# Attention with routed experts on one core: ScalarE copies 114 of 288 score half units out of PSUM

## The chip, the cores and the metric

One Trainium2 chip, one of its cores. The metric is the device time of one execution in microseconds (us). The kernel is one launch.

## The reference, cut to what matters

```python
# q, k, v: (8, 8, 576, 64) = batch, heads, tokens, head size
q_rot, k_rot = rotate(q), rotate(k)                 # rotary position
scores = 1/sqrt(64) * q_rot @ k_rot^T
attn = exp(scores - max(scores)) / (sum + 1e-9)
x = (attn @ v), heads joined                         # (8, 576, 512)
# per batch:
s = x @ w_gate                                       # one gate score a token
top = the 128 tokens with the highest s
y = relu(x[top] @ w1) @ w2                           # 512 -> 1024 -> 512
out = x;  out[top] = x[top] + sigmoid(s[top]) * y
```

## The kernel before

Work is cut into 16 **groups**: a batch and four of its eight heads. A group has 18 **half units**: `c` is one of two head pairs, `u` one of nine blocks of 64 queries. The two heads of a pair lie on the upper and lower 64 partitions, so a half unit's scores are 128 partitions x 576 keys. They fill two PSUM banks (a "wide"), 288 columns in each. There are eight banks, so at most four half units' scores stand in PSUM at a time.

For each half unit TensorE makes the scores (`units`, 16 matmuls for two half units). In `softmax` VectorE reads them out of PSUM, multiplies by -1/8, writes the negated scores to the `prob` tile in SBUF and keeps the minimum of each row in `nm`: one instruction. ScalarE then applies the exponential in place in `prob`, with the minimum as bias, and sums the rows. VectorE transposes `prob` in blocks of 32 x 32, mostly two half units at once. When all 18 half units of a group are transposed, TensorE makes the **value products** (`value`, three parts of 96 matmuls), which need four banks. Their output goes to `ot`, is transposed on TensorE, scaled by the row sums into `x`, and stored. The `prob` tile has two copies, so a group's scores can be made while the previous group's are in use.

After every second group the batch is routed: gate products on GpSimd, totals on VectorE or ScalarE, ranks of the tokens (`route`), a gather of 128 rows by indirect DMA, two expert layers on TensorE (`products`, 8 parts a batch), and an indirect DMA back. GpSimd also rotates `q_in` and `k_in`.

**Order.** Nothing is scheduled on the chip: each engine runs its instructions in a fixed order. Every operation has a number, and `LINES` holds, for each of the five queues, the numbers in order, two characters each. `Order.run` walks these five lists with its own costs to fix the order of issue and which banks each operation gets; `issue` emits the instructions with their semaphores. A bank is given to a next user when the last reader of the old one has ended. TensorE's operations have a mode (`mode` 0, 1, 2: tile shapes of 128 x 128, 32 x 64, 64 x 64); neighbours of different mode cost a change.

Line numbers in the profile are those of the helper that records every call (L236), so groups are told apart by tile names: `prob<-banks` is the read-out with the minimum, `prob<-prob,nm` the exponential, `prob<-prob` the transposition, `banks<-k_in,q_in` the scores, `banks<-prob,vt` the value products.

Of the kernel before, what the change touches and what calls it, by code (L numbers as in the profile page):

```python
# [27 lines left out]

LINES = {
    "PE": """  # L30
010P0H0X1b131j1r1x1D0T171n0-1f0L2B2R2J2F2V2x2-2N1J351K3b1L3h3n5d4L1Q4R1U1S575j4X515p5v3t3u3v6n6h6t3E3A6F3C6R6z6L6X715B4a
5C5D4h5I5K8h8n8t4k5M778z788F798R8L7i4n7e7g8X919P4r4s9V9-4u7Ia54vahab97an98at99azbP9e7Pb-bV4xc54y9i9g4z7Scb4AaFchaGcnaHct
czaOaMdl7VaQdxdr7Z7+dDcFdJcGdPcHdVflcMcOcQbe80d-81e5fr83bl84fx85bofD86fPfJebfVecf-edg5gTembrekeigZh3gbh9gchfgdhrhlgigkgm
bvhxbwiTiZbyeMbzhDj3eTbBj9bCeWjfbDjlbEhJjrhKjxhLjDkpeZhQhUhSkNkHkBkvjJkTjKkZjLl3mpjQf1jSjUf2l9mviif4mBf5mNmHf7ipf8mTf9is
famZlfn3lgn9lhnXlmivlolqnfo1ngo7nhojodnolQnqnmizopiAoviCpXiDoBlXiFq1iGoHl+iHq7iIqdoNqjoOqpoPqvqBoWoUoYm1qHrlm5rrm6rDrxpm
m8rJm9rPrVqNr-qOs5qPptmbqUqWmcqYpwsbscsdmdsisksmpzmepDsxpGpEsEpJsHpHpKpLsKpMsOsPsRsUsSsVsWsX""",
    "ACT": """
02030R0J0Z1d151l1t1v1B1F1z0V19111p1H1h0N2D2L1O2T2H2X2Z2z312P3339373f3d1M1N3j3l3p3r1R3y1V1T4N594T5h5f5n5l4P4-4Z5t1+5r4V5b
5z55535x203w3x5G226p6r6j3B6l3F6J3D6x6V6H3K6T6N3M6Z6v3O6-6P756D6B735E5F5J8r8x7c8p4p8l8j8v8B8D8H8J5U7b7a4o5W8V8N8P8T8Z957o
8-9T934t7q7s9ca39X9R4wa1a79Zafarapajada99b9aavax9faBaDc3al9jc7aKc1bXbZbR9qcfbT7Xcdc9cjclcpcraJaIcxaPcD7WdpcvdBcBdzdn7-dv  # L40
cKdtdHdFdNaYdLdTdRcJcIdXa+cPdZcRfpcW82e3fncYe1e9fte7egfvfBfzbtfHc+fFfTfLfNfRfZfXg3g1eeefg9g7enbselg-gXggh1gVh7h5hdhbeuew
hhhjgfgehvhthphnglhBgsiVgui-j1bAiXhHhzhFj7jdjbe-j5jjhOjpjhjnjvjtjBjzhNhMjHjFe+hTktkLkJkDkRkPkrkzkFkxkVjOk-l1jNjMkXl7i0l5
jTmtf3mzmxlbldmrj+f6mDmFmRk0lkmJmLmVmPn1m-ixmXn5n7nbndljlinkiwnZn-lwlAo3o5o9obnjninpofoholnniBonoxotozorp-iEpZnwoDoFoLoJ
nyoSqbqfm3q5q9qhq3qlqnqtqroRoQqzqxoXm2qDqFp2rpp4rnqLrvm7rzqJqSrtrFrLmarNrHrZrBrXrRs1s3s9rTs7qQqRqZqVr2sgpBser4pApFpIsMsT""",
    "DVE": """
0r0s0v0w0t0u0z0x0A0y0C0Q0I0Y0S1c140+1k160K1m1e1s1u1y1A1w1E1G180U1o101g1C0M0W1I1a1q2C0O2S1i2K2G2Y2W122y322U2O302M2E2+3836
2Q2A342I3e3c3a3g3k3i3q3o1P5e5g4O3s4M4U4S3m585a3z5k5m4Y4+54525s5q5o5w5y5i5u505c4W4Q566q6o6k6i6w6s6u6G6I5A6m6S6U6A6C6O6M6+
6Y74725H6W496K4e6y4d4c4g706Q4f6E4i765L8k8i8o8q8w5N8u4l7d8s5S8m8C8A8y8G8I8E4q8K8U8S8O7j8M7f7h8+8Y948Q9Q9S9290969Y9Wa07Ha2
8W7M7Na8a67L7O7Kaiak9+aeaca4aq9dao9UasagauawaaaCaAbQbS7Qc0bYbWaEc2c8c6ay9ham9occceb+7T4Bc4bUckcgci9scacocqcmcsaLcwcucCaN
cAdoaR7YdmdAcydudydsaWcEdCdGdEdqdIdMdKdwdSdQdOdUcLdWdYfobdfmcNbibhd+e0e2bjbkbge8fsfue4e6bmfqeafyehfwbpfAfGfE87fSbufMfKfQ  # L50
fIfCfWfYfUf+g2g0fOg4g8g6gUgWgaejg+h0esh4h6h2hahcgYh8hghihehkeLhuhsghhogjhmgnhwhqhyhAbxiWj0iUi+eSeQeReOePgwhEhGj6j4eUj2iY
jahCjcjgeXjihIjojebFjmf0j8jkjujsjqjAjyhPjwjCjGjEkskqjIhVhRkQkOkKkIkEkCkykwkMh+kSkWkUkGjPkuk+l0kAl2l6l4mskYjRjVi2mqihl8lc
lamymwikimiliniomCmEmumQmAmIlemKiqirmMmOmUmWk2itllfbm+mSn0mGn4n6mYn2nanciyn8nenYlnlrn+lpo2o4lyo0o8lPoaocomokognloelSlWnr
lUlTlVoioso6owoyoqoop+pYoAoCoEoulYq0q4oGoKoIl-q2oMq8qaiJqeqgnAqcqmqkq6qiqsqqoTqoquqyqwqEqCoZoVqAqIqKroqGrmrsrup6rqplrGrE
rArypspppoprrMrKpqqMrSrQrYrIrWm4rwr+s0s2rOs8qTrCs6s4purUsaqXpxshsfsjsnr6soslspsqsssrswpCmfszsDsAsCsBsFsGsIsLpNsQsNsY""",
    "POOL": """
0B0F0D0E0G2p2v2q2t2w2u2r2s4D4E4J4F4G4H4K4I6f696g1Z6a6b6d1-6c6e218b898a8c3J8d3L3N8f8e9H8g4b9L4j5R9M9N4m5T9O9I5V9J9K7n7p7r
7JbHbNbJbLbIbKbMbO7Rddde9n9pdjdh9rdi7UdfdgdkaVfjfk4CfdfeaXfffhfifgaZcVbfcXcZbnbqgNgOgLgPgRgSgQgM88eretiRiPeviLiQiNiOiMiS
greNgtgveVknkoeYkhkjkiklkmkkbGmhhZmnmimjmkmomlmmh-i1ijjZj-k1nRnVnSiunPnTnUnQnWfcpRlvlxlzpSpTpUpVlRpPpQpWnvlZnxnzm0rjrdrk
rfiKrhrergrip1p3p5pnpvr1r3pyr5symgsJpOsZ""",  # L60
    "SP": """
04060508070a090c0b0n0m0k0e0j2i0h0q0p0g2f0o0d3-2g0l232c2k26282a25240f29413X0i2j2d272b422n403V3Q3W3Y3S003P2m2l2o3R3T3U5+43
5-5X5Y5Z2h631X3Z6144483+601W62461Y453I7t7u477x3H7y7A64657w7z66685O7v3G672e7B7D7C5P7E5Q7l7k9u9A9y9z9v9t9w9C9x7F7m7G9E9D9G
9Bb0b3a-9Fb6b1b4b2b59kb7ba9l9mbbb9bcb8d2d6d5d0c-d7d1d3aUaTd4dcaSeFdad8cTcSeGezdbeAexeDd9cUeEeCeyeBeHeKeIgDgCgBgEeJgyeqgz
gxepgAgKgIgHiceogGgJgFi7iai9i4gqi5i6i3i8goieibiggpk4k3kak5k9k6kbifidhWk7k8kclKlJjXhYlDlBkflHlIlEkglCkehXkdlFjWlGlOlNnFnD
nElLlMnInCnHnBnGjYnJltpfnLntpgnKlunOnMlspepdnNpap8p7p9pbpcp0phpinso-r7pjpknur8rar9rcrbr0o+stq-q+susv""",
}


# [951 lines left out]
```

## Time and profile before

| | us |
|---|---|
| time, median of 3 runs | 520.5 (520.34 to 521.34) |
| the profiled execution's own time | 521.84 |
| its span (first to last instruction) | 520.1 |
| TensorE busy | 486.8 (94%) |
| VectorE busy | 453.1 (87%) |
| ScalarE busy | 327.1 (63%) |
| GpSimd busy | 340.3 (65%) |

PE is TensorE's matmuls, PEld its weight loads, DVE is VectorE, ACT ScalarE, POOL GpSimd, SP the engine that issues most DMAs. The end of a matmul is modelled, so a busy PE is not PE at its peak. The duration of an instruction holds its latency: the next one on the same engine can begin before it ends, so what one costs is read from start to start.

### The profile page before, as it was taken

The page shows a single profiled execution, that of the slowest core. Times are in us where ns is not written, and L with a number is a line of the kernel's source. Part 1 is how long each engine was busy: PE and PEld are TensorE (multiplying, and loading weights), DVE is VectorE, ACT ScalarE, POOL GpSimd, SP SyncE. Part 2 cuts the span into 40 slices and gives each one's busy share as a digit, 9 for nine tenths or more (in the row PEclk, how much of TensorE's full clock was granted, in tenths as well). Part 3 has the DMA queues.
Part 4 walks back from the last instruction along what each step waited for, and adds up shares of the span by engine and source line. Part 5 has one row for each costly group of instructions (what it writes and reads, how often), then busy time and mean ns, then how long its engine had stood idle before and what let it go on. Part 6 is the DMA issues. An engine that isn't in the chain of part 4 may idle for free. (4 is left out here: it accounts for less than half of the span.)

```text
span 520.1 us, 18964 instructions
## 1 busy us (share of the span) xinstructions
PE 486.8 (94%) x7988; PEld 300.1 (58%) x7988; DVE 453.1 (87%) x988; ACT 327.1 (63%) x965; POOL 340.3 (65%) x268
## 2 busy tenths in 40 slices
PE   8779897899999999999899998999999999999995
PEld 7336354455665456655557454574657556666873
DVE  7999999998998999999989989999959989992710
ACT  0666898847847768685686657775657668764000
POOL 3989299698495889658687597727778397014110
PEclk9999999899999999999999999999999999999999
DMA  8884567367545465254452547246464243121310
GB/s 293 273 249 139 176 208 232 105 186 219 162 134 150 128 177 192 84 171 140 159 167 80 182 133 226 74 119 191 149 203 120 69 149 114 52 64 49 107 41 20
DMA packets 47381, 76.52 MB, mean 147 GB/s; under 512 B 4928, under 2 KB 28224, under 8 KB 47296
## 3 DMA queue, kind: packets, MB, share of 16 engines
q1 hardware_dynamic: 45472, 70.54, 44.2%
q0 software_dynamic: 1280, 4.20, 2.3%
q8 instruction: 62, 1.02, 0.9%
q10 hardware_dynamic: 544, 0.59, 0.4%
q14 instruction: 23, 0.19, 0.2%
HBM read 63.77 MB, written 11.53 MB: 145 GB/s over the span
## 5 line engine op out<-in xcount | busy, mean ns | idle before, releaser
L236 ACT ACTIVATE prob<-prob,nm 128x576 f32<-128x576 f32 x288 | 221.1, 772 | 115.1 <-DVE prob L236 114.8
L236 DVE TENSOR_SCALAR_CACHE_REDUCE prob<-banks 128x576 f32<-128x576 f32 x288 | 204.3, 745 | 16.1 <-PE banks L236 14.1
L236 PE MATMUL banks<-k_in,q_in 64*64 64x288 f32 x2304 | 181.9, 417 | 22.5 <-DVE prob L236 8.9
L236 DVE STREAM_TRANSPOSE prob<-prob 128x1152 f32<-128x1152 f32 (+1 forms) x153 | 193.7, 1287 | 5.7 <-ACT prob L236 5.6
L236 PE MATMUL banks<-prob,vt 32*64 32x288 f32 x4608 | 150.9, 405 | 2.4 <-ACT prob L236 0.9
L236 PEld LDWEIGHTS banks<-k_in,q_in 64*64 64x64 f32 x2304 | 81.8, 133 | 109.4 <-DVE prob L236 28.7
L236 PEld LDWEIGHTS banks<-prob,vt 32*64 32x64 f32 x4608 | 98.9, 132 | 51.5 <-issue 12.6
L236 POOL TENSOR_TENSOR k_in<-k_in,tabk 128x1152 f32<-128x1152 f32 (+1 forms) x31 | 80.9, 2613 | 17.7 <-DMA k_in<-k_dram 15.1
L236 POOL TENSOR_TENSOR q_in<-q_in,tabk 128x1152 f32<-128x1152 f32 (+1 forms) x32 | 82.8, 2592 | 12.6 <-DMA q_in<-q_dram 12.4
L236 POOL TENSOR_TENSOR prod<-x,wg 128x512 f32<-128x512 f32 (+1 forms) x45 | 49.3, 1096 | 53.4 <-ACT prod L236 32.8
L236 PEld LDWEIGHTS banks<-xt,w1t 128*128 128x128 f32 x512 | 59.5, 192 | 7.9 <-issue 5.8
L236 PE MATMUL banks<-xt,w1t 128*128 128x128 f32 x512 | 63.1, 278 | 0.1
L236 PE MATMUL banks<-w2t,ht 128*128 128x512 f32 x128 | 61.9, 610 | 0.3 <-ACT ht L236 0.3
L236 ACT ACTIVATION_READ_ACCUMULATOR prob<-prob,nm 128x1 f32 x288 | 55.6, 193 | 0.0
L236 POOL TENSOR_SCALAR sel<-slots,rank 128x128 bf16<-128x128 bf16 x30 | 17.7, 603 | 43.0 <-DVE rank L236 43.0
L236 POOL TENSOR_TENSOR q_in<-q_in 128x576 f32<-128x576 f32 x31 | 44.0, 1421 | 0.9
L236 POOL TENSOR_TENSOR k_in<-k_in 128x576 f32<-128x576 f32 x31 | 43.9, 1419 | 0.8
L236 ACT ACTIVATE x<-banks,rs 128x64 f32<-128x64 f32 (+1 forms) x152 | 33.1, 326 | 9.7 <-issue 5.5
L236 PEld LDWEIGHTS banks<-w2t,ht 128*128 128x128 f32 x128 | 22.0, 189 | 23.3 <-issue 22.0
L236 ACT ACTIVATE prod<-prod 128x256 f32<-128x256 f32 (+1 forms) x56 | 22.7, 410 | 8.6 <-POOL prod L236 8.6
L236 ACT COPY ot<-banks 128x576 f32<-128x576 f32 x31 | 18.3, 640 | 15.3 <-PE banks L236 15.3
L236 ACT ACTIVATE ht<-banks 128x512 f32<-128x512 f32 x14 | 8.4, 602 | 27.3 <-PE banks L236 27.1
(67 smaller groups left out, 251.4 us busy)
## 6 DMA issues: line engine op xcount, KB each, us to landing
k_in<-k_dram SPq DMA_DIRECT2D x64, 288.0 KB, 3.8
vt<-v_dram SPq DMA_DIRECT2D x96, 192.0 KB, 3.0
q_in<-q_dram SPq DMA_DIRECT2D x62, 288.0 KB, 3.5
out_dram<-x SPq DMA_DIRECT2D x32, 256.0 KB, 2.8
w2t<-w_dram SPq DMA_DIRECT2D x8, 256.0 KB, 3.7
w1t<-w_dram SPq DMA_DIRECT2D x8, 256.0 KB, 3.7
out_dram<-x SPq DMA_DIRECT2D x16, 64.0 KB, 2.2
tabk<-rope_dram ACTq DMA_DIRECT2D x2, 288.0 KB, 4.1
```

What stands on the lines that cost most here:

```text
L236: i = made(*args, **kwargs)
```

## The change

A table `DRAINS` marks each half unit with V or S. For V everything is as before. For S ScalarE copies the scores, times -1/8, from PSUM to `prob`, and VectorE then takes the row minimum by a reduction over `prob` in SBUF; the exponential follows as before. The banks of an S half unit are read by ScalarE alone. 114 of the 288 half units are S: 8, 14, 5, 5, 9, 9, 9, 5, 10, 4, 6, 5, 3, 8, 6 and 8 in groups 0 to 15. The five order lists are made anew. Decoded, they keep every operation except the split ones; three gate totals and one copy to `ot` go from VectorE to ScalarE, one expert copy from ScalarE to VectorE. TensorE's list has the same 346 operations, with few in other places.

```diff
+    DRAINS = (
+        ("VVVVVSVSS", "SSSVVSSVV"),
+        ("VSSSSSSSS", "SSSVSVSVS"),
+        ("SVVVVVVSS", "VVSVVSVVV"),
...
+        ("VVSVVSVVS", "SVVSSSSVV"),
+    )
...
         def softmax(c, u, o, b):
             i = c * NU + u
             dst = prob.tile[:, i]
-            m = op({"DVE": dve(S, 1, 12.0)},
-                   lambda: nc.vector.tensor_scalar(
-                       dst.rearrange("p (n c) -> p n c", n=2), bank_of(b)[:, :, 0:HALF], -(D ** -0.5), None, op0=ALU.mult, op1=ALU.min,
-                       accum_out=nm.tile[:, i:i + 1]),
-                   [o] + nm.before + prob.before, b)
+            wide = dst.rearrange("p (n c) -> p n c", n=2)
+            least = nm.tile[:, i:i + 1]
+
+            def taken():
+                nc.vector.tensor_scalar(
+                    wide, bank_of(b)[:, :, 0:HALF], -(D ** -0.5), None, op0=ALU.mult, op1=ALU.min, accum_out=least)
+
+            def drained():
+                nc.scalar.mul(wide, bank_of(b)[:, :, 0:HALF], -(D ** -0.5))
+
+            def lowest():
+                nc.vector.tensor_reduce(least, dst, axis=AX.X, op=ALU.min)
+
+            if DRAINS[g][c][u] == "V":
+                m = op({"DVE": dve(S, 1, 12.0)}, taken, [o] + nm.before + prob.before, b)
+            else:
+                d = op({"ACT": act(S)}, drained, [o] + prob.before, b)
+                m = op({"DVE": dve(S)}, lowest, [d] + nm.before)
+                prob.by(d)
             x = op({"ACT": (760, 870)},
```

## Rows read from the trace of the kernel before

**Rows 1.** The page, part 1: busy us, share, instructions.
```profile
PE 486.8 (94%) x7988; PEld 300.1 (58%) x7988; DVE 453.1 (87%) x988; ACT 327.1 (63%) x965; POOL 340.3 (65%) x268
```

**Rows 2.** Busy time by stretch: length, then each engine.
```profile
10.00:42.00 32.00, 25.00 (x230) 12.27 (x234) 32.00 (x71) 19.49 (x51) 29.00 (x16) 1.00 0.85 271
42.00:72.00 30.00, 26.55 (x522) 14.40 (x526) 29.98 (x67) 23.68 (x72) 19.36 (x11) 1.00 0.51 156
72.00:99.00 27.00, 22.45 (x448) 12.82 (x431) 25.99 (x48) 23.59 (x81) 23.42 (x15) 0.94 0.62 186
99.00:117.00 18.00, 16.94 (x395) 10.75 (x403) 17.82 (x38) 11.06 (x33) 16.40 (x17) 1.00 0.59 178
117.00:301.00 184.00, 178.40 (x3030) 108.56 (x3021) 173.03 (x364) 130.28 (x387) 135.81 (x106) 1.00 0.51 154
301.00:470.00 169.00, 164.31 (x2868) 101.45 (x2853) 154.38 (x331) 109.39 (x315) 105.11 (x82) 1.00 0.42 125
470.00:520.00 50.00, 44.59 (x507) 31.62 (x505) 13.66 (x52) 8.29 (x31) 9.67 (x14) 1.00 0.17 57
```

**Rows 3.** Waits of the whole span: us in total, times, longest.
```profile
ACT prob L236 <- DVE prob L236: 114.8, 74, 9.6
...
PEld banks L236 <- DVE prob L236: 40.0, 70, 2.3
...
DVE prob L236 <- PE banks L236: 14.1, 28, 2.7
...
PE banks L236 <- DVE prob L236: 9.7, 22, 1.9
```

**Rows 4.** Timeline, VectorE: three instructions in a row (start, duration).
```profile
201.13 0.75 DVE L236 TENSOR_SCALAR_CACHE_REDUCE prob<-banks 128x576 f32<-128x576 f32 x1
...
201.81 0.68 DVE L236 TENSOR_REDUCE gp<-prod 128x2 f32<-128x512 f32 x1
...
202.41 2.63 DVE L236 STREAM_TRANSPOSE prob<-prob 128x1152 f32<-128x1152 f32 x2
```

**Rows 5.** Groups by form: count, busy us, mean ns, idle before.
```profile
L236 ACT ACTIVATE prob<-prob,nm 128x576 f32<-128x576 f32 x288 | 221.1, 772 | 115.1 <-DVE prob L236 114.8
...
L236 ACT COPY ot<-banks 128x576 f32<-128x576 f32 x31 | 18.3, 640 | 15.3 <-PE banks L236 15.3
...
L236 DVE TENSOR_REDUCE gp<-prod 128x2 f32<-128x512 f32 x6 | 4.0, 666 | 1.8 <-POOL prod L236 1.7
...
L236 DVE TENSOR_REDUCE gp<-prod 64x1 f32<-64x256 f32 x7 | 2.8, 405 | 0.0
```

**Rows 6.** Timeline, ScalarE: two copies of 128x576 from PSUM in a row.
```profile
80.63 1.18 ACT L236 COPY ot<-banks 128x576 f32<-128x576 f32 x2 [0.78 <-PE banks L236]
```

**Rows 7.** Timeline, weight loads: gap with and without a change of mode.
```profile
208.21 2.66 PEld L236 LDWEIGHTS banks<-prob,vt 32*64 32x64 f32 x96 [0.44 <-issue]
...
466.65 0.19 PEld L236 LDWEIGHTS banks<-w2t,ht 128*128 128x128 f32 x1 [0.24 <-issue]
```

**Rows 8.** Timelines: last transpositions, first value products, groups 0 to 3.
```profile
39.66 0.76 DVE L236 STREAM_TRANSPOSE prob<-prob 128x576 f32<-128x576 f32 x1
...
41.85 3.17 PE L236 MATMUL banks<-prob,vt 32*64 32x288 f32 x96 [0.58 <-issue]
...
63.01 1.37 DVE L236 STREAM_TRANSPOSE prob<-prob 128x1152 f32<-128x1152 f32 x1
...
71.54 8.99 PE L236 MATMUL banks<-prob,vt 32*64 32x288 f32 x288 [0.16 <-DVE prob L236]
...
89.66 2.64 DVE L236 STREAM_TRANSPOSE prob<-prob 128x1152 f32<-128x1152 f32 x2
...
98.94 2.44 PE L236 MATMUL banks<-prob,vt 32*64 32x288 f32 x72 [0.15 <-DVE prob L236]
...
110.66 1.37 DVE L236 STREAM_TRANSPOSE prob<-prob 128x1152 f32<-128x1152 f32 x1
...
116.33 1.96 PE L236 MATMUL banks<-prob,vt 32*64 32x288 f32 x56 [0.30 <-DVE prob L236]
```

More of the change, by code (lines that the diff above doesn't have):

```diff
@@ L30 @@
     "PE": """
[L31 to L34, printed above, removed]
@@ L35 @@
-famZlfn3lgn9lhnXlmivlolqnfo1ngo7nhojodnolQnqnmizopiAoviCpXiDoBlXiFq1iGoHl+iHq7iIqdoNqjoOqpoPqvqBoWoUoYm1qHrlm5rrm6rDrxpm
-m8rJm9rPrVqNr-qOs5qPptmbqUqWmcqYpwsbscsdmdsisksmpzmepDsxpGpEsEpJsHpHpKpLsKpMsOsPsRsUsSsVsWsX""",
-    "ACT": """
-02030R0J0Z1d151l1t1v1B1F1z0V19111p1H1h0N2D2L1O2T2H2X2Z2z312P3339373f3d1M1N3j3l3p3r1R3y1V1T4N594T5h5f5n5l4P4-4Z5t1+5r4V5b
-5z55535x203w3x5G226p6r6j3B6l3F6J3D6x6V6H3K6T6N3M6Z6v3O6-6P756D6B735E5F5J8r8x7c8p4p8l8j8v8B8D8H8J5U7b7a4o5W8V8N8P8T8Z957o
-8-9T934t7q7s9ca39X9R4wa1a79Zafarapajada99b9aavax9faBaDc3al9jc7aKc1bXbZbR9qcfbT7Xcdc9cjclcpcraJaIcxaPcD7WdpcvdBcBdzdn7-dv
@@ L41 @@
[L41 to L44, printed above, removed]
-    "DVE": """
@@ L46 @@
[L46 to L55, printed above, removed]
+010Q0H0Z1e161m1w1D1a0U111i1K1r0L312T2J362O2F3d2Y1R3l1S3s1T3A3H5B55201Y5c1+5v5I5i5p5O5V3P3Q3R6P6I6W3W3Y783+7l717e7r7x604w
@@ new lines @@
+61624D67698N8V914G6b7D997E9g7F9t9m7O4J9z7K7M9Gas4N4OaFay4Q8caN4Ra-aV9Mb69Nbc9ObkcB9T8jcPcWcJ4T8md14U9V4V9X4Wbrd8bsdgbtdn
+dtbAbyegbC8peneu8t8ueAdAeHdBeNdCeTglc0dHdJdL8we+8xgsf5c78zgz8Aca8BgF8CgVgNfbh0fch7fdhei1ficdfkfmi8ighlimhmithniFizhwhuch
+hsiLcikbk5ckfMclkiiRfTcnkpcofWkwcpkDcqiXkJiYkQiZkWlJj6j4fZj2m7m0lVlPl1mel2mll3mrlal8g1nOg2mxnUlcjwg4n+g5oao4g7jDg8ohg9jG
+gaonmEoumFoBmGpnjJmLmPmNoHpvoIpBoJpHpOoQoSndoOjNpVjOq1jQnkrvjRq8jTrBjUqennjVrHjWrOqlrVqms0qns6sdnqqwquqssjs-nut6nvtjtcnx
+qWtqnytxtFsrtMsstSstr1nAsCnBsysAtZt+r4t-nCu8u4r7u6nDrbujrercuqrhutrfrirjuwrkuAuDuBuEuGuHuIuJ""",
+    "ACT": """
@@ new lines @@
+02030S0-0J1g1n181p1z1E1B1y1I121G0V141k1L1c0M1s0X322U0O1P2K1N341u1W2P373b3h2W2Z3e3j2H392M3m2R3g3q2-3t3w3o3v1U1V3y3B3I3L5E
+3D3F3N3K21561Z1-3U5g585e5l5a5x5M5P5K5G5t5D265R5r5W5z5k5T5n5+5Y3T3S6Q286L6S6U6X3Z3-3X6N2a656K747c7f447j7p467n487h7v7z6-7a
+6Z7B7t767364637I688O8R8W8Z95926c944L8Y978-6h8Q9c8T6j9e9b9i9k7H7G6l9n4K9x9p9A9E9r9v9C7U9K9I7W4PaJaG7YaB9RawaOaRau4Sb0aAb2
+aIaLaTaDaQb8baaZbgbdaX9Q9PblbicFcCbpcScXcHbfbnb4cUcNd28rcRcEbw9WcZc-d6a1cLd9d4dca3dedjdbdidlbvbudwbBeh8qdreqdpdvdyelep8v
+ejeBewbKeydFeDeFeseLeRePdDdEeUeJgodKgneYeWf1dR8ygtdTgqf3f0dVgvf7f9gxfggBgJcfgGgDgLgWgOgRg+gIgTh3gYh2h5gQhah9hcfeffhhhgi2
@@ new lines @@
+hjflici9i4ieibikiiiphqi6irfwioixivhphoiHiJhtiBiDkehCk7iNk9hEcmkliPhGkdkgiVknksiTkrkzkuf-kyj0kkkFkHkMkBkLkOkUkSi-i+kZkYk-
+j5f+malNm1lYm9jcm5m3l6mclLlTmhlRl+mglXmnl4l5mjmtmpjglbmvg3mAldmCnSmznQlinYg6o2odmJo8o6lknWo0lmjLojocoqofopolovosoxozoDoF
+mImHprpojKmMoMpxpqmZptpFpDoKoLpIpRpKoRpzpQpZpWpMjPq4pToPq6q3p-oYrzpYrxqcqarFqfo+qhqjrKqqrRnsp0rJrMrDrQrTrWr+rYs2s4qoqps7
+sbs9qxnrsfskqCsnt2qEsht1t4nwtmqGt8tdsmtotattspnztBtytltItftvtAtDswtHthtstQtKtTtVtOsvtXsuu2szsBsIu0u1r9r8rduyrguxuC""",
+    "DVE": """
@@ new lines @@
+0r0s0v0w0t0u0x0z0y0A0C0R0I0+0T1f17100K1o1h191q1x1A1H1F1b1C131j1O1J0W150N1l1M1t0Y331d2V1Q3a0P1v2G38351X3i2+2L2Q2I3f3p2X3n
+3c3k2S3u3x3r303E3z3C5C3M3J595F3O5f5d573G5w5y5J5L2N5j5s5q5S5h5m5Z5Q5N5H5b5A5X5U5o6T6R3V6J6M6+5u6V797b5-7o7m726O7i7s7u667g
+6Y7y7A4v7q757k4C4y4B4A4z7w704E7d6a7C8P774H8X937J968S8+4M989a909d8U9h9j9f9l9u9w9q7P9o9D7L7N9H9B9Jat9Fav9L9saH8baz9S9yaC8h
+8g8f8i8eb3aSb1aWaYaKaxb9aPb7aMaEaUbha+bbbobm9U8kcGcQcDbecKcMcYcTc+8nbjb5d3bqd59YcI4Xd0cVcOd7dddabxdhdka5dfdmdodudqbz8sek
+eibDdxeoevexbIdsdzeEemeCerezeIeKbMeGeteQb-eOdGeSeXeVgmc2dIc5c6gpdMc3eMe-c4eZf2gwf6f8c8gugrf4gAgygCcbfhfagKcg8DgZgEgPgHgS
@@ new lines @@
+gXgMh1h4g-h6h8hbgUhdhfhii5fjcefnhki3idiaihijfsiffuiqinili7hriwiuisiyiIfLiGhxiAiCiKhviOiMcjiEkck6k8kffOfSfPfRfQkjkmfUiUka
+khiSkqktiWiQkxfXkEkGkvj1kAcrkIkKkNkokCkTkRg0kPkVkXk+lKlMj7j3l0m8m4lWlQm2lSmblZm6mfmdjemilOmmmolUl7l-msmumkmqnRl9nPmwmyjv
+mBnXnVjyjzjAn-o1jBjCmDobnTo7o5jEjFo9oeoiokmKjHnZgbooo3orogjMoyowomotoAoCoEoGmOmQmVpwmXpyoNpspppEncpCpupGpLpJpPninfoTngnj
+pSnhpAp+pNpXq5q2pUnlryrwq7qbjSq0q9rErAqdnoqiqgrCrIqkjXrPrSqrrLrNrGrZrUrXs1s3r-s5sas8sesgqvqtsct0slsot3t9t7sit5nttktgqVte
+tnq-qYtrqZq+r0tusqtGtCtztbtJtptNtPtEtitWtUtLtRsxtwr2tYsDr5sKu3rau9u5u7sMuauducubueuiuounnEumulupurusuuuzrluFuK""",
@@ L56 @@
     "POOL": """
[L57 to L60, printed above, removed]
+0B0F0E0D0G2B2D2C2E2z2A2x2y4Z4+4-53545051526G6H6A256B6C6E276F6D8J8F298H8I438K45478G8Lak8M4x4Fao6gaq6iar4Iam6kalanap7T7V7X
@@ L61 @@
+ctcucz8dcxcAcycvcw8le8eae9eba0eceda28oa4eeef4YbHgjbJgkgdgebLghgigfggc1dQdSdUc9h-cchXi08EhZhVh+hYhWfrk1ftk2fvk3j-k0jZk4j+
+hBhDhFfVfNlHlFfYlIlGlBlClDlEjbnGcsnMjdnKnNnLnHnInJjflhphljjxpfllpljIpggcpjpmpipkmUmWrpmYrrrqrsrtrunernrooXoZnmnpo-sZsTsU
+sVjYsXsYs+sWqBqDqFr3qXsHr6sJsLnFukuvrmuL""",
     "SP": """
-04060508070a090c0b0n0m0k0e0j2i0h0q0p0g2f0o0d3-2g0l232c2k26282a25240f29413X0i2j2d272b422n403V3Q3W3Y3S003P2m2l2o3R3T3U5+43
-5-5X5Y5Z2h631X3Z6144483+601W62461Y453I7t7u477x3H7y7A64657w7z66685O7v3G672e7B7D7C5P7E5Q7l7k9u9A9y9z9v9t9w9C9x7F7m7G9E9D9G
@@ L64 @@
-9Bb0b3a-9Fb6b1b4b2b59kb7ba9l9mbbb9bcb8d2d6d5d0c-d7d1d3aUaTd4dcaSeFdad8cTcSeGezdbeAexeDd9cUeEeCeyeBeHeKeIgDgCgBgEeJgyeqgz
-gxepgAgKgIgHiceogGgJgFi7iai9i4gqi5i6i3i8goieibiggpk4k3kak5k9k6kbifidhWk7k8kclKlJjXhYlDlBkflHlIlEkglCkehXkdlFjWlGlOlNnFnD
-nElLlMnInCnHnBnGjYnJltpfnLntpgnKlunOnMlspepdnNpap8p7p9pbpcp0phpinso-r7pjpknur8rar9rcrbr0o+stq-q+susv""",
+04060507080a090c0p0b0m0f000d0o0n0e0g0q0l4m4l2o0j0h0k2b2h0i2k2c2s2r2d2e2j2i2f2n4i4k2g2l2u4o2v4p2w4f2q4g494h4a4b4c4d2t4n4e
+4q2p6r6q6m6p242m4u6n6v6o6s4s236u4r6t224t84837Z7+7-4j6w8281406z86426x416f806y856dabada7af88a6acaa7R7S87a98a89a86eae7QbVag
@@ L67 @@
+bObNbQbPbRbUbSaiajbWah9ZbTbZ9+9-e2e3e1e0dZd-dWdXbYbXd+dYbGb+e4fFe5bEe7dNbFdPfEfAfDfBfze6fxfCdOfyfGfJfKfHhLhMfIhOhNhIfphJ
+hShKhPhHjphUjqfohThyhRfqhzjojnjmhQjljjjkjijhjsjrjujthAlvlnlolsltlulplrj8lyjaj9lqn0n1n5lgm+n7m-n2lzn4lxlwn3lAn9n8n6p5p3p6
+p4nbnap9p1pbmTlep7p8lfpapepcqPp2pdmSmRqNqOqHqIqKoUqJqLqMoWqAsNqQsOqTqSqyoVqRsQqUsSqzsRsPuhsGufsFsEug""",
 }
@@ L463, in attention_moe_kernel @@
     APART = {0: 6, 1: 3}
+    DRAINS = (
+        ("VVVVVSVSS", "SSSVVSSVV"),
+        ("VSSSSSSSS", "SSSVSVSVS"),
+        ("SVVVVVVSS", "VVSVVSVVV"),
+        ("VSSVVSVVV", "SVVSVVVVV"),
+        ("SSSVVSVSV", "SSSSVVVVV"),
+        ("VVSSVSVSS", "VSSSVVVSV"),
+        ("SVVSSSVVV", "SVSVVSSVS"),
+        ("SVVSVVSVV", "VSVVVVVSV"),
+        ("VSVSSSVVV", "SVVSSVSSS"),
+        ("SSVVVVVVV", "VSVSVVVVV"),
+        ("VVVVVVVVV", "VSSSSVSVS"),
+        ("VVVSVVVVV", "VVSVSSVVS"),
+        ("VVVVVVVSV", "VVVVSVSVV"),
+        ("SVVSVSVVS", "SVVVSSSVV"),
+        ("VVVVSVSVS", "VVSSVVVVS"),
+        ("VVSVVSVVS", "SVVSSSSVV"),
+    )
     loaded, vals, rotated = {}, {}, {}
```

## The prediction

> **What bounds the kernel now.** I read the busy line first [rows 1]: TensorE is busy 94% of the span, VectorE 87%, ScalarE 63%. No engine is the bound by that alone, so I cut the span into stretches at the marks where the value products of a group begin [rows 2]. From 10 to 72 us VectorE is busy 61.98 of 62.00 us and TensorE only 51.55. From 72 to 117 VectorE has 43.81 of 45, TensorE 39.39. From 117 to 470 both are nearly full: TensorE 342.71 and VectorE 327.41 of 353. After 470 TensorE works off the deferred experts, with 44.59 of 50. So TensorE's idle time in the body (10 to 470) is 32 + 30 + 27 + 18 + 184 + 169 = 460 less 433.65, which is 26.4 us, and 16.1 of that falls before 117. VectorE's idle time in the body is 460 less 433.2, 26.8 us, nearly all of it after 117.
>
> The waits say what these gaps are [rows 3]. TensorE's matmuls stood 9.7 us and its weight loads 40.0 us (70 times) before the scores' banks until a VectorE instruction on `prob` had ended: the bank was full, and VectorE had not yet read it out. Of 40.0, up to 70 x 0.44 = 31 is no stall, since a load that nothing holds up shows 0.44 us after a change of tile shape too [rows 7]. VectorE in its turn stood 14.1 us for TensorE's scores. ScalarE stood 114.8 us for VectorE: it has the room.
>
> The marks show that VectorE's total is not what TensorE is late for [rows 8]. Group 0's value products begin at 41.85, 1.4 us after the transposition that they need (39.66 + 0.76). But group 1's begin at 71.54, though its last transposition ended at 63.01 + 1.37 = 64.38: 7.2 us of lag. Group 2's begin at 98.94; its last transposition is the first of the pair that starts at 89.66 and ends about 91.0: 7.9 us. Group 3's begin at 116.33 after 110.66 + 1.37 = 112.03: 4.3 us. In those lags TensorE was still pushing score units of the next group through banks that were slow to come free. That lag is what a second reader of the banks can shorten.
>
> **The change, part by part.**
>
> *VectorE's instruction.* Three instructions in a row give the slots from start to start: the fused multiply-and-minimum from PSUM holds VectorE 201.81 - 201.13 = 0.68 us, and a reduction of 512 columns in SBUF 202.41 - 201.81 = 0.60 [rows 4]. The reductions of 512 and 256 columns last 666 and 405 ns on average [rows 5], 1.02 ns a column, so 576 columns take 0.60 + 64 x 1.02 ns = 0.665 us. The gain is 0.015 us x 114 = 1.7 us of VectorE, practically nothing. Bounds: 0.60 (no dearer than 512 columns), -9 us; and 0.73 if the result's latency is exposed each time (0.666 + 0.065), +6 us. I take 0.665, the slot of the nearest row.
>
> [...]
>
> *ScalarE's copy.* Not in the trace as such; the nearest row is the copy of the same 128x576 from two banks into `ot`, 640 ns [rows 5], and two in a row take 1.18 us, so a slot is 0.54 [rows 6]. 114 x 0.54 = 62 us; at 0.77, the exponential's mean [rows 5], it would be 88. ScalarE goes from 327 to about 389 us of 520, 75%. This is off the path while ScalarE has slack: 12.5 of 32 us idle in 10 to 42, 6.3 of 30 in 42 to 72, but only 3.4 of 27 in 72 to 99 [rows 2]. The `DRAINS` table puts 8 and 14 copies into groups 0 and 1 and only 5 and 5 into groups 2 and 3, so most of the early 32 (17 us) fall where there is room.
>
> *Latency of a half unit.* A copied one reaches its exponential a copy (0.64) later than before. Its exponential and transposition are needed when the value products begin, and the lags of 7.2, 7.9 and 4.3 us cover that. Group 0 has only 1.4 us of cover; there the price would be up to 0.64 us.
>
> *Banks.* This is the point. A copied half unit's banks come free after ScalarE's 0.64 us, whatever VectorE is doing; the reduction is queued on VectorE later, from SBUF, and holds no bank.
>
> *The order tables.* TensorE's sequence is almost the old one. It changes tile shape 186 times instead of 182: 4 x (0.44 - 0.24, the gap of a load with and without a change [rows 7]) = 0.8 us more. Ahead of a group's last transposition VectorE now has 21 softmax instructions in group 0 (was 24), 46 in group 1 (42), 61 in group 2 (62), 73 in group 3 (72), 94 in group 4 (96), and 288 in the last. Three of the gate totals and one copy move from VectorE to ScalarE, one expert copy the other way: 3 x 0.60 and about 0, so VectorE is 2 us lighter and ScalarE 3 us heavier, neither where it ends last. SP's and GpSimd's queues keep all their work; no load is added, and they are reordered only to follow.
>
> **The sum**, mark by mark. A group's value products can begin no sooner than its transpositions (VectorE's order) and than TensorE gets there.
>
> - Group 0: three softmax slots fewer ahead, 3 x 0.68 = 2.0 us sooner.
> - Group 1: TensorE idles 3.45 us in 42 to 72 [rows 2]. I let half of it go, since 19 of the 36 half units of groups 1 and 2 are copied: 1.7. Sooner by 3.7, at 67.8. Its transpositions end at 64.38 + 4 x 0.68 = 67.1 at worst, so this just fits.
> - Group 2: idle 4.55 in 72 to 99, half is 2.3: sooner by 6.0, at 92.9, after 91.0. Fits.
> - Group 3: its transpositions have one more softmax ahead (+0.7) and VectorE's idle time in 72 to 117 is 1.2 us, so they end at 111.5 to 112.7. TensorE cannot use all its lead: about 4.3 sooner. VectorE's pace takes the rest back.
> - 117 to 470: TensorE idles 10.3 us; half, 5.2, goes. VectorE must follow, which takes 5.2 + 4.3 of its 25.6 us of idle time there. It mostly stood for TensorE's scores, so it can.
> - After 470: the same deferred products in the same order on TensorE: 0.
>
> -4.3 - 5.2 + 0.8 = -8.7. The profiled execution took 521.84 us (span 520.1, 1.7 outside it), 0.26% above the median of 520.5, so 513.1 against it, and 511.8 against the median. Matmul ends are modelled, so a busy TensorE hides some of its standing and 26.4 is a lower bound of the stalls; for that I take **511.0 us**.
>
> **The rivals.**
>
> *A bigger gain.* Nearly all of the 26.4 us goes, VectorE's idle time with it, because both engines get looser at once. For it: VectorE idles 26.8 us and mostly for TensorE. Against it: up to 72 VectorE has no idle time at all, and its work is not less. Limit 520.5 - 26.4 + 0.8 = 495; typically 498 to 505.
>
> *No change.* VectorE's pace sets the scores' pace; a bank freed early is followed by a reduction of the same length, and TensorE merely waits at the value products instead of at the banks. For it: 61.98 of 62 us busy. Against it: lags of 7 us at two marks. 520 to 521. [...]
>
> *Slower: the minimum waits for ScalarE's queue.* A copy is queued behind exponentials that wait for VectorE's minimum, the minimum behind it waits for the copy, and everything on VectorE behind that, transpositions too, stands. Place: 42 to 117, where ScalarE was busy 23.68 + 23.59 + 11.06 of 75 us and VectorE has no slack. Price: 24 copies of groups 1 to 3; if each keeps VectorE standing one exponential (0.77), 18 us, less the 4.3 won: 534. It decides from 4.3 / 24 = 0.18 us of standing per copy, and over the whole body from (9.5 + 25.6) / 114 = 0.3 us. For it: ScalarE has only 75 - 58.3 = 16.7 us free there and the copies take 24 x 0.54 = 13. Against it: part of group 1's copies come before 42, where 12.5 us are free, and the lags allow some standing. Likely 522 to 530.
>
> *The copy does not do what it says*, being dearer than the `ot` row: at 0.77 ScalarE has 415 us, still under TensorE; it would cost part of the gain and end at 515 to 519.
>
> **How the numbers follow.** Forecast (505 to 515) 0.53; bigger gain 0.17; a small gain (515 to 519) 0.11; no change 0.07; slower 0.12. The range leaves out the slower case, no change and the outer part of the bigger gain: 501 to 519. Faster by over 0.2% (under 519.5, about what a measurement of this kernel can tell) 0.81, within 0.2% 0.07, slower 0.12.
>
> **What would show it.** Right: the copy near 0.64 us, a reduction near 0.73 with slots of 0.66; ScalarE about 390 us, VectorE within 10 us of 453; TensorE's waits for VectorE on the scores' banks clearly down before 117; value products of groups 1, 2, 3 beginning near 68, 93, 112; TensorE's busy time unchanged, its idle time 8 to 10 us less. Wrong: VectorE idle before 90 us with "ScalarE prob" as releaser (the queue rival); the marks where they were (no change); or marks that keep gaining after 117 by more than 5 us (bigger gain).

## The result and the profile after

The changed kernel takes 514.93 us, the median of 4 runs (514.89 to 516.16), against 520.51 (520.34 to 521.34, 4 runs) for the kernel before: a ratio of 0.9895 [0.9877, 0.9913], 5.6 us less. The forecast was 511.0, or 9.5 less. The direction holds, one term of the sum is too large, and the mechanism is borne out in part. The profiled execution after took 514.91 us with a span of 513.2; that of before took 521.84 with 520.1.

The page, part 1, answers to [rows 1]:

```profile
PE 484.9 (94%) x7988; PEld 301.1 (59%) x7988; DVE 449.5 (88%) x871; ACT 389.8 (76%) x1087; POOL 340.8 (66%) x268
```

ScalarE went from 327.1 to 389.8 us, VectorE from 453.1 to 449.5, and TensorE's work stayed. The stretches of [rows 2] again, after the change (columns: length, then the busy time of PE, PEld, DVE, ACT, POOL; then the granted clock, DMA share, GB/s):

```profile
10.00:42.00 32.00, 26.61 (x254) 13.85 (x258) 31.40 (x57) 25.34 (x61) 29.74 (x16) 0.95 0.76 250
42.00:72.00 30.00, 25.50 (x498) 13.59 (x490) 29.69 (x53) 29.07 (x81) 21.34 (x12) 1.00 0.67 201
72.00:99.00 27.00, 22.99 (x490) 14.00 (x482) 26.45 (x45) 26.95 (x89) 21.55 (x14) 0.94 0.65 187
99.00:117.00 18.00, 16.56 (x427) 10.85 (x419) 17.84 (x35) 17.57 (x52) 16.84 (x17) 1.00 0.64 191
117.00:301.00 184.00, 180.31 (x3083) 109.82 (x3075) 175.77 (x325) 153.25 (x421) 139.44 (x108) 1.00 0.51 153
301.00:470.00 169.00, 166.71 (x2979) 104.32 (x2971) 149.93 (x291) 131.91 (x378) 102.09 (x82) 1.00 0.40 123
```

From 117 to 470 TensorE idles 6.0 us instead of 10.3. From 10 to 117 its idle time hardly fell: 107 less 91.66 is 15.3, after 16.1. There the other two engines tell why: from 42 to 117 VectorE is busy 73.98 of 75 us, as before, and ScalarE 73.59, where it had 58.33.

The waits of the whole span, which answer to [rows 3] (us in total, times, longest):

```profile
ACT prob L238 <- DVE prob L238: 29.4, 18, 10.2
ACT prob L238 <- PE banks L238: 22.5, 34, 2.3
PEld banks L238 <- ACT prob L238: 21.7, 42, 1.8
...
PEld banks L238 <- DVE prob L238: 14.3, 23, 1.6
...
DVE prob L238 <- PE banks L238: 11.2, 27, 0.9
```

The weight loads' wait for VectorE fell from 40.0 us to 14.3, and 21.7 us of wait for ScalarE came up in its place: 36.0 together. ScalarE's wait for VectorE fell from 114.8 to 29.4.

Groups by form, the instructions of the change (count, busy us, mean ns, idle before):

```profile
L238 ACT ACTIVATE prob<-prob,nm 128x576 f32<-128x576 f32 x288 | 220.7, 771 | 39.9 <-DVE prob L238 29.4 <-DVE nm L238 9.8
...
L238 DVE TENSOR_SCALAR_CACHE_REDUCE prob<-banks 128x576 f32<-128x576 f32 x174 | 125.8, 742 | 11.9 <-PE banks L238 11.2 <-ACT prob L238 0.2
...
L238 DVE TENSOR_REDUCE nm<-prob 128x1 f32<-128x576 f32 x114 | 81.5, 732 | 0.2
L238 ACT ACTIVATE prob<-banks 128x576 f32<-128x576 f32 x114 | 71.5, 647 | 22.9 <-PE banks L238 22.5
```

The last two rows are the new pair: a copy of 647 ns, a reduction of 732. VectorE stood 0.2 us in all before the 114 reductions: hardly ever did it find a copy late.

The marks, as in [rows 8]: the first value products of groups 0 to 3 and 15 after the change:

```profile
41.14 2.20 PE L238 MATMUL banks<-prob,vt 32*64 32x288 f32 x64
...
71.73 1.67 PE L238 MATMUL banks<-prob,vt 32*64 32x288 f32 x42
...
97.65 1.72 PE L238 MATMUL banks<-prob,vt 32*64 32x288 f32 x48
...
114.46 1.94 PE L238 MATMUL banks<-prob,vt 32*64 32x288 f32 x53 [0.32 <-ACT prob L238]
...
463.16 1.23 PE L238 MATMUL banks<-prob,vt 32*64 32x288 f32 x32
```

Against 41.85, 71.54, 98.94 and 116.33 [rows 8], and 470.51 for group 15 of the kernel before, the marks of groups 0 to 3 are sooner by 0.7, -0.2, 1.3 and 1.9 us, and group 15's by 7.35. So 1.9 us were won up to group 3, 5.5 from there to group 15, and 0.4 were lost behind it: the last matmul ended at 507.88 instead of 514.84, 7.0 sooner.

### The profile page after: what moved, and what is told of

Its sections match the earlier page's. It is cut to its first block, busy times and chain, and to the rows that moved or that the text cites. A ratio compares the mean times of both kernels' runs of the same rounds, so it can differ in the third digit from the quotient of the medians.

```text
span 513.2 us, 19024 instructions
## 1 busy us (share of the span) xinstructions
PE 484.9 (94%) x7988; PEld 301.1 (59%) x7988; DVE 449.5 (88%) x871; ACT 389.8 (76%) x1087; POOL 340.8 (66%) x268
## 3 DMA queue, kind: packets, MB, share of 16 engines
q8 instruction: 62, 1.02, 0.8%
## 4 chain that ended last, share of the span: by engine, by line
PE 64%; ACT 12%; POOL 8%; issue 7%; DVE 6%; DMA 2%; SPq 1%; POOLq 0%; DVEq 0%
PE banks L238 64%; ACT prob L238 7%; DVE prob L238 5%; POOL k_in L238 4%; POOL q_in L238 3%; ACT ot L238 2%; ACT x L238 2%; DMA k_in<-k_dram 2%; SPq L238 1%; POOL prod L238 1%; ACT rs L238 0%; DVE nm L238 0%; ACT prod L238 0%; POOLq L1050 0%; POOL xe L238 0%
## 5 line engine op out<-in xcount | busy, mean ns | idle before, releaser
L238 ACT ACTIVATE prob<-prob,nm 128x576 f32<-128x576 f32 x288 | 220.7, 771 | 39.9 <-DVE prob L238 29.4
L238 PEld LDWEIGHTS banks<-k_in,q_in 64*64 64x64 f32 x2304 | 83.5, 134 | 101.3 <-issue 25.4
L238 DVE TENSOR_SCALAR_CACHE_REDUCE prob<-banks 128x576 f32<-128x576 f32 x174 | 125.8, 742 | 11.9 <-PE banks L238 11.2
L238 POOL TENSOR_TENSOR q_in<-q_in,tabk 128x1152 f32<-128x1152 f32 (+1 forms) x32 | 82.8, 2592 | 15.3 <-DMA q_in<-q_dram 15.2
L238 ACT ACTIVATE prob<-banks 128x576 f32<-128x576 f32 x114 | 71.5, 647 | 22.9 <-PE banks L238 22.5
L238 DVE TENSOR_REDUCE nm<-prob 128x1 f32<-128x576 f32 x114 | 81.5, 732 | 0.2
```

The source lines that it names most:

```text
L238: i = made(*args, **kwargs)
```

## The experiments

Theory A: the gain is banks that ScalarE frees while VectorE's queue is elsewhere (this the prediction holds), and the early part of it is cut by ScalarE, which the copies fill from 42 to 117 (this the profile after suggests). Rivals: B, the gain is the order that was made with the choice, whoever reads the bank; C, the copies' worth is less work on VectorE; D, the early gain is lost at another place, GpSimd's rotations. The kernels ran in three sets, each on its own chip, and each set has its own runs of the kernel before (523.62, 521.27 and 521.66 us), so ratios are compared. In the diffs - is the changed kernel and + the experiment.

### The copies without the new order: old_order and old_order_hold

`old_order` keeps the 114 copies and reductions, but all lists are the old ones: the copy is put into ScalarE's list where the old read-out began, the reduction where VectorE's read-out stood. Only `LINES` differs, here the last line of GpSimd's list:

```diff
-sVjYsXsYs+sWqBqDqFr3qXsHr6sJsLnFukuvrmuL""",
+sVjYsXsUsWsYqBqDqFqXr3sHsJr6sLuknFuvrmuL""",
```

> The 114 copies and reductions, but in the order of the kernel before: each copy stands in ScalarE's list where the old read-out began, each reduction at the old read-out's place on VectorE; the other lists are the old ones. If banks that come free early are the gain, with any order that leaves ScalarE room: 514 to 518 us. If the gain is the new order: 520 or more, since each minimum now waits for a copy (0.64 us) that the old order does not allow for; up to 530.

Measured: 588.53 us, ratio 1.123 [1.1202, 1.1258], far above both ranges. The waits of that kernel show the queue rival of the prediction at work:

```profile
ACT prob L238 <- DVE prob L238: 63.1, 42, 8.2
...
DVE nm L238 <- ACT prob L238: 58.8, 69, 3.0
...
ACT prob L238 <- DVE nm L238: 37.3, 32, 4.8
```

VectorE stands 58.8 us before 69 of the reductions until ScalarE's copy has ended, and ScalarE stands for VectorE in turn. In the changed kernel VectorE stands 0.2 us before all reductions together. The copies alone, in an order that doesn't know them, are dear.

`old_order_hold` is the same, and gives the bank free only after the reduction:

```diff
-                m = op({"DVE": dve(S)}, lowest, [d] + nm.before)
+                m = op({"DVE": dve(S)}, lowest, [d] + nm.before, b)
```

> As the run before it, with one difference: a copied half unit's banks are given back only when VectorE's reduction has ended, not when ScalarE's copy has. If the early release is what counts: at least 4 us above that run, 522 to 535. If the release counts for nothing (the shorter slot of VectorE, or the order alone): within 1 us of it.

Measured: 586.37 us, 1.1201 [1.1176, 1.1225], the same within the intervals. Where copies and reductions of `old_order`'s trace are matched by the lists, a reduction begins 0.03 us (the median) after its copy has ended, and ends 0.8 us after it. So there is little early release to lose, and its loss cost nothing: this pair tells next to nothing of theory A.

### The order without the copies: order_only

Every half unit is V again, with VectorE's read-out where the copy began; the rest of the new order is kept, and with it which engine does what. (The moves named in "The change" are net: by the two tables 18 operations go from VectorE to ScalarE and 15 back.) The lists change with it and are not shown.

```diff
-        ("VVVVVSVSS", "SSSVVSSVV"),
-        ("VSSSSSSSS", "SSSVSVSVS"),
...
+        ("VVVVVVVVV", "VVVVVVVVV"),
+        ("VVVVVVVVV", "VVVVVVVVV"),
...
```

> The new order without copies: VectorE reads all 288 half units out of PSUM as before the change; a read-out that replaces a copy stands on VectorE where that copy began in the trace, the reduction is gone. If the order made anew is the gain: 514 to 517 us. If copies are needed for it: 520 to 526, with TensorE's waits for VectorE on the scores' banks back at 35 to 50 us of weight loads.

Measured: 541.13 us, 1.0332 [1.031, 1.0354]. Theory B falls for this order: without the copies it is 17 us slower than the kernel before it. Its waits of TensorE for VectorE:

```profile
PEld banks L237 <- DVE prob L237: 57.8, 79, 3.2
...
PE banks L237 <- DVE prob L237: 31.7, 42, 3.3
```

These were 40.0 and 9.7 [rows 3], and are 14.3 and 7.0 after the change. An order made anew for a kernel without copies was not tried, so how much of the 1% such an order would give by itself is not shown.

### The banks alone: held, v_in_l_all and its two halves

`held` has all instructions and all lists of the changed kernel. Only the release differs, and with it which banks `Order.run` hands out: for 106 of the 114 copied half units (the set `HELD`; for the other 8 the late release would have closed a circle of waits) the banks come free after the reduction.

```diff
-                m = op({"DVE": dve(S)}, lowest, [d] + nm.before)
+                m = op({"DVE": dve(S)}, lowest, [d] + nm.before, b if (g, c, u) in HELD else None)
```

> The changed kernel with the same instructions in the same order, but 106 of the 114 copied half units keep their banks until VectorE's reduction has ended (the other 8 would lock the order up). Only the time at which banks come free differs. If early banks are the gain: all of it goes and more, since the order counts on them, ratio to the kernel before 1.00 to 1.05. If the gain lies in VectorE's instruction or in the order: 0.987 to 0.992 as the changed kernel.

Measured: 618.27 us, 1.1844 [1.1815, 1.1873]. Its waits:

```profile
PEld banks L238 <- DVE nm L238: 40.7, 26, 4.7
PE banks L238 <- DVE nm L238: 37.9, 25, 4.2
```

Not an instruction is added, and TensorE's matmuls stand 37.9 us and its weight loads 40.7 (partly at the same time) for reductions; in the changed kernel there is one such stop, of 0.4 us. This is the cleanest test: the early release is what the order lives on.

`v_in_l_all` removes these 106 copies and puts the old read-out from PSUM where the reduction stood (the lists lose the copies, not shown). ScalarE loses 106 x 0.54 = 57 us of work, and the banks come free as late as in `held`.

```diff
-        ("VVVVVSVSS", "SSSVVSSVV"),
-        ("VSSSSSSSS", "SSSVSVSVS"),
...
+        ("VVVVVVVVV", "VVVVVVVVV"),
+        ("VVVVVVVVV", "VVVVVVVVV"),
...
```

> The new order, with 106 of the 114 copies taken out: VectorE's read-out from PSUM stands where its reduction stood. Banks come free as late as in the run before this one, but ScalarE has 106 x 0.54 = 57 us less to do. If banks alone matter: within 0.5% of that run. If ScalarE's fullness costs early on as well: 5 to 10 us below it, still above the changed kernel. If the order alone is the gain: 0.987 to 0.992.

Measured: 612.02 us, 1.1739 [1.1677, 1.18], 6 us under `held`. Of the (1.1844 - 0.9895) x 521.27 = 102 us that late banks cost against the changed kernel, taking 57 us off ScalarE gives back 6. The same edit on one part of the groups each:

```diff
-        ("VSSVVSVVV", "SVVSVVVVV"),
+        ("VVVVVVVVV", "VVVSVVVVV"),
```

> The changed kernel, with 31 of the 32 copies of groups 0 to 3 taken out in this way, the others kept. If the early copies cost ScalarE more than their banks win: faster than the changed kernel, ratio 0.982 to 0.988, value products of group 3 sooner than at 114. If early banks are worth more: group 3 at 117 to 125 and a ratio of 0.995 to 1.01.

`v_in_l_0to3` (31 of the 32 early copies gone, late ones kept): 538.13 us, 1.0326 [1.0299, 1.0353]. Neither of the two ranges given held it; I had thought of the early copies as nearly free to undo.

> The changed kernel, with 75 of the 82 copies of groups 4 to 15 taken out, the early ones kept. Group 3's value products begin at 114 to 115 as in the changed kernel. If the later gain of 5.5 us comes from the banks there: it goes, and more, ratio 0.997 to 1.02. If it comes from the order: 0.989 to 0.992.

`v_in_l_4to15` (75 of the 82 late copies gone, early ones kept): 586.66 us, 1.1246 [1.1222, 1.1271]. Against 0.9895 the parts cost 4.3% and 13.5%, 17.8% together, and the whole 18.4%: the banks count in both stretches, by number of copies more or less (0.14% and 0.18% each).

Most of these kernels lost far more than was expected: 588 us against at most 530 (`old_order`), 541 against 526 (`order_only`), 1.184 against 1.05 (`held`), 1.125 against 1.02 (`v_in_l_4to15`). Each of these fixed orders lost much, 3% to 18% against the kernel before, where one thing that it counts on came late. So these losses show that the order needs its early banks; they don't measure how much of the 1% is theirs.

### ScalarE's load early: double and half_exp

`double` makes each copy of groups 1 to 3 twice.

```diff
-                nc.scalar.mul(wide, bank_of(b)[:, :, 0:HALF], -(D ** -0.5))
+                for _ in range(2 if g in (1, 2, 3) else 1):
+                    nc.scalar.mul(wide, bank_of(b)[:, :, 0:HALF], -(D ** -0.5))
```

> The changed kernel, with each of the 24 copies of groups 1 to 3 made twice: 24 x 0.54 = 13 us more for ScalarE between 30 and 100 us, nothing else. If ScalarE's fullness from 42 to 117 us (73.6 of 75 busy) is what ate the early gain, it sets the pace there: the value products of group 3 begin 8 to 13 us later and the time is 519 to 527. If ScalarE is off the path there: 515 to 516.

Measured: 532.68 us, 1.0179 [1.0155, 1.0203]. Group 3's mark:

```profile
128.88 1.47 PE L238 MATMUL banks<-prob,vt 32*64 32x288 f32 x40 [0.31 <-ACT prob L238]
```

It is 14.4 us later than after the change, for 24 x 0.54 = 13 us of work; all later marks are 14.8 to 16.2 later. So in this stretch the longer copies cost all of their 13 us. A doubled copy also holds its bank 0.54 us longer, and this run can't part that from ScalarE's load.

`half_exp` does the opposite: the exponential of groups 1 to 3 runs over 288 of 576 columns, and so leaves out half of theirs.

```diff
-                       dst, dst, AF.Exp, bias=nm.tile[:, i:i + 1], scale=-1.0, accum_out=sums.tile[:, i:i + 1]),
+                       dst[:, 0:S // 2] if g in (1, 2, 3) else dst, dst[:, 0:S // 2] if g in (1, 2, 3) else dst,
+                       AF.Exp, bias=nm.tile[:, i:i + 1], scale=-1.0, accum_out=sums.tile[:, i:i + 1]),
```

> The changed kernel, with the exponential of groups 1 to 3 made over 288 of 576 columns (the rest of those probabilities is left as negated scores): 54 x 288 x 0.83 ns = 13 us less for ScalarE before 117 us. If ScalarE's fullness ate the early gain, the value products of group 3 begin 2 to 4 us sooner, with VectorE's pace as the next limit, and the ratio to the kernel before falls from 0.9895 to 0.982 to 0.986. If VectorE alone sets the pace there: unchanged within 0.2%.

Measured: 513.79 us, 0.984 [0.9809, 0.9871], barely apart from 0.9895 [0.9877, 0.9913] and within the range given for ScalarE's fullness. An exponential over 288 columns took 526 ns in its trace and one over 576 columns 771, so 0.85 ns a column (0.83 expected) and 13.2 us less for the 54. But the changed kernel was not run in this set, and the trace speaks against that reading. One window over 42 to 117, first of this kernel:

```profile
42.00:117.00 75.00, 65.54 (x1370) 38.39 (x1351) 74.09 (x133) 63.30 (x221) 60.52 (x40) 0.98 0.64 194
```

and of the changed kernel:

```profile
42.00:117.00 75.00, 65.05 (x1391) 38.44 (x1383) 73.98 (x130) 73.59 (x220) 59.73 (x41) 0.98 0.66 194
```

ScalarE has 10 us of room again, and TensorE gets 0.5 us more done: VectorE is as full as it was. The marks of groups 0 to 3 stand at 39.82, 70.27, 96.08 and 112.90, which is 1.3 to 1.6 sooner than after the change, but already at group 0, and `double_late` below, whose program is the changed kernel's up to group 7's value products and which ran on the same chip as `half_exp`, shows the same early marks in its profile:

```profile
39.92 1.47 PE L238 MATMUL banks<-prob,vt 32*64 32x288 f32 x40
...
70.50 1.71 PE L238 MATMUL banks<-prob,vt 32*64 32x288 f32 x48
...
96.03 2.20 PE L238 MATMUL banks<-prob,vt 32*64 32x288 f32 x64
...
113.01 2.39 PE L238 MATMUL banks<-prob,vt 32*64 32x288 f32 x65 [0.32 <-ACT prob L238]
```

Two profiles of one early program lie 1.2 to 1.6 us apart from the first mark on. Against the second of them the half exponential won 0.1 us at group 3. So theory A's second half isn't borne out: room on ScalarE alone didn't quicken the stretch from 42 to 117, where VectorE is full.

### ScalarE's load late: double_late

The same doubling for groups 9 to 13, where ScalarE has room (26 copies, 14.0 us).

```diff
-                nc.scalar.mul(wide, bank_of(b)[:, :, 0:HALF], -(D ** -0.5))
+                for _ in range(2 if g in (9, 10, 11, 12, 13) else 1):
+                    nc.scalar.mul(wide, bank_of(b)[:, :, 0:HALF], -(D ** -0.5))
```

> The changed kernel, with each of the 26 copies of groups 9 to 13 made twice: 26 x 0.54 = 14 us more for ScalarE between 240 and 410 us. If ScalarE has room there (285.2 of 353 us busy after 117): less than 4 us more, ratio 0.990 to 0.997. If its queue is on the path there as well: 8 to 14 us more, 1.005 to 1.017.

Measured: 524.64 us, 1.0061 [1.0044, 1.0078], so (1.0061 - 0.9895) x 521.66 = 8.7 us more than the changed kernel. Group 15's mark in its trace:

```profile
471.49 0.74 PE L238 MATMUL banks<-prob,vt 32*64 32x288 f32 x16
```

That is 8.3 later than after the change, or 9.8 with the 1.45 by which its group 3 was sooner: 0.7 us for each us added, though ScalarE is busy only 131.91 of 169 us from 301 to 470 in the changed kernel. So late too, room on ScalarE didn't make these copies free. Whether it is the added work or the bank, which a doubled copy holds 0.54 us longer, this run can't tell.

### VectorE's work: short_min

The 114 reductions read 64 of 576 columns, and so leave out most of the minimum. VectorE loses 60 us of work (in its trace such a reduction takes 202 ns, in the changed kernel's 732); the banks and the order are those of the changed kernel.

```diff
-                nc.vector.tensor_reduce(least, dst, axis=AX.X, op=ALU.min)
+                nc.vector.tensor_reduce(least, dst[:, 0:64], axis=AX.X, op=ALU.min)
```

> The changed kernel, with each of the 114 reductions over 64 of 576 columns (the minimum of the rest is left out): 114 x 512 x 1.02 ns = 60 us less for VectorE, the order kept. If VectorE's work still sets the pace in the body: 8 to 15 us less, ratio 0.961 to 0.975. If TensorE and ScalarE do: 0 to 4 us, 0.982 to 0.990.

Measured: 514.76 us, 0.9865 [0.9835, 0.9894], at most a few tenths of a per cent below the changed kernel. The window 42 to 117:

```profile
42.00:117.00 75.00, 65.00 (x1383) 37.63 (x1367) 62.20 (x131) 73.48 (x221) 58.15 (x40) 0.98 0.62 188
```

VectorE has 12.8 us of room, ScalarE is full, TensorE does no more than before. Beside `half_exp` this says that in this stretch both engines are at their limit, and easing one of them wins nothing. Theory C falls too: VectorE's busy time fell by only 3.6 us with the change, and 60 us less work on VectorE are worth 1.6 us by the ratios, whose intervals overlap, and 1.1 by the end of the last matmul. Easing both at once wasn't tried.

### GpSimd's rotations: short_rot

After the change TensorE's longest early stop for GpSimd is this one:

```profile
34.45 6.76 PE L238 MATMUL banks<-k_in,q_in 64*64 64x288 f32 x56 [2.82 <-POOL k_in L238]
```

`short_rot` rotates the third and fourth pair over half of the columns (the other half is left as it came).

```diff
+                hi = S // 2 if pi in (2, 3) else hi
```

> The changed kernel, with the rotations of the third and fourth pair on GpSimd over 288 of 576 columns (the other columns stay as loaded): 8 us less for GpSimd before 40 us. TensorE's stall of 2.98 us at 34.45, behind the rotated k_in, goes and group 0's value products begin 0.5 to 1.5 us sooner than at 41.14. If ScalarE and VectorE set the pace from there: group 3 within 0.7 us of 114.5, ratio 0.987 to 0.990. If the early gain was lost at the rotation: group 3 at 111 to 113, ratio 0.983 to 0.987.

Measured: 515.02 us, 0.9871 [0.9843, 0.9899]. The stop is gone, and a stop of the same length stands a few us later, now for ScalarE:

```profile
38.62 3.42 PE L238 MATMUL banks<-k_in,q_in 64*64 64x288 f32 x24 [2.54 <-ACT prob L238]
```

Group 0's mark came at 43.33, later and not sooner, in a profile of 517.28 us. By the time theory D falls, though the ratio lies on the border of its two ranges (0.983 to 0.987 and 0.987 to 0.990); why this profile was late isn't known. None of the kernels that compute everything was faster than the changed one.

## Why the prediction was right, and where its size was off

**The sum.** Forecast were -4.3 by group 3, -5.2 + 0.8 from there to group 15, and 0 behind: -8.7 on the profiled time. Measured: -1.9, -5.5 and +0.4, together -7.0 on the trace (514.91 against 521.84). Of the 3.9 us between the forecast of 511.0 and 514.93, 2.4 are the first term; the second came out 1.1 better, the last 0.4 worse. The other 2.2 are reference points: 0.8 was my step from 511.8 to 511.0 for standing hidden in a busy TensorE, which nothing bore out, and 1.35 because the profiled execution of before lay 1.3 us above its median and that of after did not. TensorE's idle time from 10 to 470 fell by 5.1 us, from 26.4 to 21.3, where 8 to 10 stood as the sign of being right.

**The mis-sized term: groups 0 to 3.** Of its four steps group 0 is right within what two profiles differ by (2.0 forecast, 0.7 measured, 1.9 in the profile of `double_late`). Group 1 is where it failed: "I let half of it go" and "so this just fits". Its last transposition did end near the 67.1 worked out from four slots more on VectorE (68.46, and 67.24 in `double_late`), but the value products came 3.26 us behind it in both, at 71.73 and 70.50 for 67.8 forecast. The lag fell from 7.2 to 3.3 because the transposition went later, not the mark sooner. TensorE's idle time from 42 to 72 did not halve, it rose from 3.45 to 4.50 us. The stops of its matmuls from 42 to 117, before and then after:

```profile
PE banks L236 <- DVE prob L236: 3.9, 12, 0.6
PE banks L236 <- ACT x L236: 3.8, 3, 2.0
...
PE banks L238 <- DVE prob L238: 5.1, 8, 1.8
PE banks L238 <- ACT ot L238: 2.2, 3, 1.2
PE banks L238 <- ACT x L238: 1.9, 3, 1.2
```

The matmuls' stops for VectorE's read-outs were to shrink and grew. (Those of the weight loads fell from 11.9 to 5.0 us, and 5.8 us of waits for ScalarE on `prob` came up beside them.) The copies don't take work from VectorE, so with 73.80 of 75 us busy before it had 1.2 us to give, and gave next to nothing; that is the reasoning of the "no change" rival, and in this stretch it holds. The sum used it for group 3 alone ("VectorE's pace takes the rest back"), and should have used it for groups 1 and 2 as well. It is not VectorE's pace alone: in `short_min`, where VectorE has room and ScalarE is full, group 1's mark stands at 71.77. For group 3 the sum has 112.0; measured 114.46, or 113.01 in `double_late`.

**The late term** has about the right size: half of TensorE's 10.3 us of idle time was to go, and 4.3 went. VectorE followed, as forecast, and keeps slack there (325.70 busy of 353). That the order needs its early banks there, `held` and `v_in_l_4to15` show. But the prediction took these idle times for waits for VectorE's read-outs, and most were not. The stops of TensorE's matmuls from group 3's mark to group 15's, in the windows 116.33 to 470.51 before and 114.46 to 463.16 after:

```profile
PE banks L236 <- ACT ot L236: 3.2, 10, 0.9
PE banks L236 <- DVE x L236: 1.5, 2, 1.1
PE banks L236 <- DVE prob L236: 1.4, 5, 0.4
...
PE banks L238 <- ACT ot L238: 2.4, 10, 0.3
PE banks L238 <- ACT prob L238: 2.0, 3, 1.3
```

Read-outs were 1.4 of the 10.3 us. These stops are gone after the change, and so are those for VectorE's scaling into `x`, while TensorE stands more for ScalarE on `prob` (0.9 us, then 2.0). That the half came out is in part luck, and what share of the late gain is the copies' and what share the other places and moves of the new order is not shown. "Marks that keep gaining after 117 by more than 5 us" stood as a sign of the bigger gain; they gained 5.5, just past it, but VectorE's and TensorE's early idle time didn't go, so the rival falls.

**The prices** hold. The copy took 647 ns (forecast 640), and ScalarE's busy time came to 389.8 (about 390). The reduction took 732 ns (about 730). The slots, read from start to start in the timeline of VectorE:

```profile
56.14 0.71 DVE L238 TENSOR_REDUCE nm<-prob 128x1 f32<-128x576 f32 x1
56.77 0.75 DVE L238 TENSOR_SCALAR_CACHE_REDUCE prob<-banks 128x576 f32<-128x576 f32 x1
...
57.45 1.41 DVE L238 TENSOR_REDUCE nm<-prob 128x1 f32<-128x576 f32 x2
58.77 0.75 DVE L238 TENSOR_SCALAR_CACHE_REDUCE prob<-banks 128x576 f32<-128x576 f32 x1
```

A reduction holds VectorE 0.63 us here and (58.77 - 57.45) / 2 = 0.66 there, the fused read-out 0.68, near the 0.665 and 0.68 of the sum. So the reduction was 0.02 to 0.05 us shorter, where the sum has 0.015.

**The rivals.** The queue rival's price was not paid: VectorE stood 0.2 us before the reductions. In the new order a reduction begins 1.1 us (the median) after its copy has ended; in `old_order`, where the median is 0.03, the price shows (58.8 us). Its remark that ScalarE had "only 16.7 us free" from 42 to 117 was worth more than the prediction made of it: 15.3 of them were used, `double` shows that copies longer by one more us cost a full one, and `half_exp` that the last did not. "Off the path while ScalarE has slack" was too kind for the late stretch as well: there 14.0 us more of copies cost 9.8, with slack all around.
